# In the attention stage, the written order of the instructions is kept on two queues instead of five

## The chip, the cores and the metric

One core of one Trainium2 chip runs the whole program. The metric is the device time of one execution in microseconds (us); every time below is from that core. A core has five engines, each with an in-order queue: TensorE (PE in the profile; PEld is its weight load), VectorE (DVE), ScalarE (ACT), GpSimd (POOL) and SyncE (SP, which here only issues DMAs). An instruction at the head of a queue that waits for something holds everything behind it on that engine.

## The reference

Three steps follow one another. First a linear attention with random features (4 sequences of 576 tokens, 8 heads of 64, 128 features); then a mixture of experts that routes each token to one of 8 experts; then a gated FFN (SiLU of one product times another, times a third matrix). Cut to what matters:

```
phi(x): proj = x @ omega.T;  h = proj - sum(x*x)/2;  exp(h - max(h)) / sqrt(128)
kv = sum_s k_p[s] v[s];  z = sum_s k_p[s]
attention = (q_p @ kv) / (q_p @ z + 1e-6)
logits = normalise(x) @ normalise(expert_emb).T / tau;  idx = argmax;  gate = softmax(logits)[idx]
moe = gate * relu(x @ w1[idx]) @ w2[idx]
out = (silu(moe @ w_gate) * (moe @ w_val)) @ w_out
```

## The kernel before, in words

The 2304 tokens are 18 tiles of 128. The attention runs over 36 **units** (the list `units`, line 358), one tile of k or of q each: units 0 to 8 are nine k tiles, 9 to 17 the nine q tiles of the same two sequences (group 0), 18 to 26 and 27 to 35 the same for the other two sequences (group 1). A unit goes through these helpers:

- `load`: a DMA of the tile, 512 KB, from SP's queue. Four buffers, so the load of unit s+4 waits for the projection of unit s.
- `squares` (L391, for most q tiles also two halving adds L396, all on GpSimd), `norms` (L403, a sum on VectorE). Three `sq` buffers: the squares of a unit wait for the L403 three units before.
- `project` (L411, TensorE, 16 small matmuls into one of two PSUM pairs named `two`), `maxima` (L421 the maximum over PSUM, then the two short steps L425 and L428 in SBUF that make the bias; all on VectorE), `exps` (L437, eight activations on ScalarE, which then free the PSUM pair).
- k units then do `kv_sum` (L451, TensorE). q units do `turn` (L485, eight transposes into two PSUM banks `one`), `turned` (L490, one copy of a bank on VectorE and one on ScalarE), `numerators` (L503, TensorE, bank `third`, which needs both copies), `divide` (L514, L517, L518, VectorE; frees `third`), `token_norms` (L527, ScalarE), `turn_x` (L532, four transposes into a bank `one`, then the cast L535 on ScalarE) and `turned_x` (L539, VectorE).
- For every third q tile a piece of the router: `products` (L218), `products_out` (L225), `logits` (L230 into `third` in units 20 and 23, copied out by L233 on VectorE). Then, spread over the units by a generator that is advanced once a unit: the roots (L144 to L159, L210, L211), the softmax and gates (L242 to L272), and the counts (L288 to L307), which end in the index of the first expert (L300, `dom_i`).

The loop over `s` (lines 573 to 625) writes these stages down software-pipelined: in step s stand `turned`, `numerators` and `divide` of unit s-2, `turn_x` of unit s-3, `turn` or `kv_sum` of unit s-1, and the projection, maxima and exps of unit s itself. In the last steps it also fetches the first expert's weights (`first.fetch`, line 625): a DMA into `raw` whose address is read from `dom_i`, the cast L89 on ScalarE and the subtraction L90 on GpSimd. All of it lies in `tc.manual_schedule()`: inside it every engine issues its instructions in the order of the source. Outside it a list scheduler orders each engine, by its own estimates; the expert's matmuls (L671, then L691), which are written after the block, may be put between instructions of the block wherever the scheduler finds their inputs early enough. After the attention come the experts (to about 375 us) and the gated FFN (L865, L838).

Of the kernel before, what the change touches and what calls it, by code (L numbers as in the profile page):

```python
# [27 lines left out]
def attention_moe_ffn_kernel(  # L28
# [40 lines left out]
    def third():  # L69
        return psum.tile([128, 2, 512], F32, tag="third", name="third", bufs=1)  # L70
# [244 lines left out]
    ENG = mybir.EngineType  # L315
# [49 lines left out]
    with p1:  # L365
# [193 lines left out]

        with tc.manual_schedule():
            p = third()
            for _ in range(13):
                nc.tensor.matmul(p[:, 0, 0:128], ones, ones, start=True, stop=True)
# [386 lines left out]
```

## Time and profile before

| | |
|---|---|
| median of 3 runs | 823.15 us (822.75 to 823.5) |
| the profiled execution, its own time | 824.23 us |
| its span on the chip, first to last instruction | 822.5 us |
| busy: PE, PEld | 802.4 us (98%), 707.4 us (86%) |
| busy: DVE, ACT, POOL | 533.1 us (65%), 273.1 us (33%), 165.8 us (20%) |
| mean granted TensorE clock | 0.993 |

How to read it: busy time is the sum over the instructions of an engine. PE is busy nearly throughout, but a matmul that is fed slowly by a waiting weight also counts as busy, so a busy PE can still be held by another engine. The rows of the section before the prediction come from views of the trace: busy time in stretches, who waited for whom (the time an engine sat idle, its times, the longest), and the timeline (start, duration, engine, line, operation, output<-input, and in brackets the idle time before it and what ended it).

### The profile page before, as it was taken

Reading aid. Unit: us, or ns where it says so; the run is one execution under the profiler, and the core shown is the slowest. Engines: PE = TensorE matmul, PEld = TensorE weight load, DVE = VectorE, ACT = ScalarE, POOL = GpSimd, SP = SyncE. Lnnn points to the kernel's source line nnn. Section 1 sums busy time; section 2 is a strip of 40 time slices with the busy share of each in tenths; the row PEclk is TensorE's granted clock in tenths of the full one; section 3 lists DMA queues with packets and bytes.
Section 4 is the critical chain, followed back from the end, with each engine's and each line's share of the span. In section 5 each row is a group of like instructions: output and inputs, shape, how many; then the busy total and the mean of one; then the engine's idle time right before and its main releaser. Section 6 shows DMA issues by size and latency. Waiting matters only on the chain.

```text
span 822.5 us, 13988 instructions
## 1 busy us (share of the span) xinstructions
PE 802.4 (98%) x5734; PEld 707.4 (86%) x5735; DVE 533.1 (65%) x917; ACT 273.1 (33%) x628; POOL 165.8 (20%) x163
## 2 busy tenths in 40 slices
PE   8989989999999998999999999999999999999998
PEld 7778867899999998998888888888888888888886
DVE  5888899684333432689992059728954993797354
ACT  3678577642222324322224232112211221221120
POOL 4452253120000004412232111212111121112020
PEclk9999999999999998999999999999999999999999
DMA  7745652132423241332120002101110210020014
GB/s 282 210 115 174 185 170 72 61 117 82 100 92 92 79 92 55 103 93 87 53 76 26 1 27 77 52 1 52 51 52 1 78 55 22 26 78 26 1 52 179
DMA packets 23680, 66.71 MB, mean 81 GB/s; under 512 B 3104, under 2 KB 5680, under 8 KB 23608
## 3 DMA queue, kind: packets, MB, share of 16 engines
q1 hardware_dynamic: 23608, 65.74, 26.1%
q8 instruction: 46, 0.75, 0.4%
q14 instruction: 26, 0.21, 0.1%
HBM read 60.94 MB, written 4.79 MB: 80 GB/s over the span
## 4 chain that ended last, share of the span: by engine, by line
PE 60%; DVE 0%; issue 0%
PE two L865 24%; PE one L838 18%; PE third L865 12%; PE two L671 3%; PE third L691 2%; PE two L691 2%; PE third L671 1%; DVE y_acc L847 0%
## 5 line engine op out<-in xcount | busy, mean ns | idle before, releaser
L865 PE MATMUL two<-xp,wp 128*128 128x512 f32 (+1 forms) x960 | 209.5, 368 | 0.0
L865 PEld LDWEIGHTS two<-xp,wp 128*128 128x128 f32 x960 | 168.1, 188 | 31.4 <-DVE s L872 0.6
L838 PE MATMUL one<-wo,h 128*128 128x512 f32 x648 | 159.8, 390 | 0.0
L90 POOL TENSOR_TENSOR h<-s,h 128x512 fp32r<-128x512 f32 (+1 forms) x60 | 78.1, 1302 | 337.9 <-ACT h L89 337.9
L838 PEld LDWEIGHTS one<-wo,h 128*128 128x128 f32 x648 | 120.6, 188 | 24.8 <-DVE y_acc L847 0.3
L847 DVE TENSOR_TENSOR y_acc<-y_acc,one 128x512 f32<-128x512 f32 x90 | 61.5, 684 | 77.3 <-PE one L838 77.2
L865 PE MATMUL third<-xp,wp 128*128 128x512 f32 (+1 forms) x480 | 106.5, 368 | 0.0
L865 PEld LDWEIGHTS third<-xp,wp 128*128 128x128 f32 x480 | 84.4, 188 | 15.4
L437 ACT ACTIVATE ph<-two,bias 128x128 f32<-128x128 f32 x288 | 78.1, 384 | 33.6 <-DVE bias L428 26.2
L671 PE MATMUL two<-xp,wp 128*128 128x288 f32 x576 | 82.7, 302 | 3.7 <-DVEq L756 3.7
L671 PEld LDWEIGHTS two<-xp,wp 128*128 128x128 f32 x576 | 80.1, 194 | 4.0 <-ACT xp L89 3.9
L89 ACT CAST h<-s 128x512 fp32r<-128x512 f32 (+1 forms) x60 | 34.7, 579 | 77.7 <-DVE s L872 77.7
L89 ACT CAST wp<-raw 128x1024 fp32r<-128x1024 f32 x32 | 33.6, 1049 | 61.8 <-PE two L691 35.1
L872 DVE TENSOR_TENSOR s<-two,s 128x512 f32<-128x512 f32 (+1 forms) x40 | 25.3, 633 | 44.3 <-ACT s L871 44.2
L691 PE MATMUL third<-h,wp 128*128 128x288 f32 x384 | 52.5, 296 | 0.0
L691 PE MATMUL two<-h,wp 128*128 128x288 f32 x384 | 51.8, 296 | 0.0
L871 ACT ACTIVATE s<-two 128x512 f32<-128x512 f32 (+1 forms) x40 | 22.1, 552 | 89.0 <-PE two L865 89.0
L691 PEld LDWEIGHTS third<-h,wp 128*128 128x128 f32 x384 | 51.6, 189 | 0.0
L691 PEld LDWEIGHTS two<-h,wp 128*128 128x128 f32 x384 | 51.4, 189 | 0.0
L90 DVE TENSOR_TENSOR wp<-raw,wp 128x1024 fp32r<-128x1024 f32 x30 | 39.6, 1319 | 14.9 <-ACT wp L89 14.9
L90 POOL TENSOR_TENSOR xp<-y_f,xp 128x576 fp32r<-128x576 f32 x12 | 18.6, 1590 | 151.3 <-ACT xp L89 151.3
L421 DVE TENSOR_REDUCE mx<-two 128x8 f32<-128x1024 f32 x36 | 43.8, 1216 | 5.2 <-PE two L411 5.0
(150 smaller groups left out, 925.9 us busy)
## 6 DMA issues: line engine op xcount, KB each, us to landing
raw<-in_w_dram SPq DMA_DIRECT2D x68, 512.0 KB, 3.6
q<-in_qx_dram SPq DMA_DIRECT2D x18, 512.0 KB, 3.6
k<-in_kx_dram SPq DMA_DIRECT2D x17, 512.0 KB, 4.1
v<-in_vx_dram SPq DMA_DIRECT2D x18, 276.0 KB, 3.8
out_dram<-y_acc SPq DMA_DIRECT2D x18, 256.0 KB, 2.0
gate<-gts SPq DMA_DIRECT2D x4, 256.0 KB, 5.3
k<-in_kx_dram SPq DMA_DIRECT2D x2, 128.0 KB, 2.2
k<-in_kx_dram SPq DMA_DIRECT2D x1, 256.0 KB
```

The source lines that it names most:

```text
L89: nc.scalar.copy(hi, src)
L90: lo_eng.tensor_tensor(out=lo, in0=src, in1=hi.bitcast(F32), op=ALU.subtract)
L421: nc.vector.tensor_reduce(out=mx.rearrange("p (c a) -> p a c", a=2), in_=p.rearrange("p a (h m) -> p a h m", m=M), axis=AX.X, op=ALU.max,)
L437: nc.scalar.activation(out=ph[:, h, :], in_=p[:, h % 2, h // 2 * M:(h // 2 + 1) * M], func=AF.Exp, bias=bias[:, h:h + 1],)
L671: nc.tensor.matmul(ps[:, j], w[:, a, c, f * 128:(f + 1) * 128], xp[:, c, b, c0 + j * HB:c0 + (j + 1) * HB], start=(c == 0 and n == 0), sto ...
L691: nc.tensor.matmul(ps[:, j], w[:, a, f, :], h[:, b, j * HB:(j + 1) * HB], start=(f == 0 and n == 0), stop=(f == len(hs) - 1 and n == 2),)
L838: nc.tensor.matmul(p, h[:, x, i * 128:(i + 1) * 128], w[:, a, :], start=(k == 0), stop=(k == 3 * GF - 1),)
L847: nc.vector.tensor_tensor(out=dst, in0=dst, in1=p, op=ALU.add)
L865: nc.tensor.matmul(ps[:, m], w[:, a, m, c, :], xp[:, c, x, cols], start=(k == 0), stop=(k == 3 * NC - 1),)
L871: nc.scalar.activation(out=s, in_=ps[:, 0], func=AF.Silu)
L872: nc.vector.tensor_tensor(out=s, in0=ps[:, 1], in1=s, op=ALU.mult)
```

## The change

```diff
-        with tc.manual_schedule():
+        with tc.manual_schedule(engines={ENG.PE, ENG.SP}):
             p = third()
             for _ in range(13):
                 nc.tensor.matmul(p[:, 0, 0:128], ones, ones, start=True, stop=True)
```

Inside the block TensorE's and SP's instructions keep the order of the source; those of ScalarE, VectorE and GpSimd are now placed by the list scheduler. The instructions themselves are the same. SP's order does not change at all, and TensorE's first change stands behind the projection of unit 35: from there on the first expert's matmuls (L671) stand earlier and in other places between the last units' steps. There is one other thing in that stretch: the last `turn_x` (unit 35) now stands directly behind the numerators of the same unit and three small L230, where before 21 matmuls L671 stood between. Three places show what moves. A name's number is the buffer; `ph` are the exps' outputs, `qt` the copies of a turned tile, `x` the divided tile, `mx` and `bias` the maxima and the exps' bias, `sh` the norms, `wp` and `raw` the expert's weights.

ScalarE at the first q unit (unit 9; `qt_691` is its copy, `ph_670` and `ph_714` are the exps of units 10 and 11). Before:

```order
L475 ACTIVATE kv1_646<-third_434 128x260
L437 ACTIVATE ph_670<-two_654,bias_666 128x128 x8
L490 COPY qt_691<-one_680 128x512
L437 ACTIVATE ph_714<-two_698,bias_710 128x128 x8
L490 COPY qt_757<-one_746 128x512
```

and with the change:

```order
L475 ACTIVATE kv1_646<-third_434 128x260
L490 COPY qt_691<-one_680 128x512
L437 ACTIVATE ph_670<-two_654,bias_666 128x128 x8
L437 ACTIVATE ph_714<-two_698,bias_710 128x128 x8
L490 COPY qt_757<-one_746 128x512
```

The copy of unit 9 now stands ahead of the exps of unit 10; that of unit 10 stays behind the exps of unit 11. The same is done at unit 27.

VectorE in a q unit (unit 14: `mx_940`; `one_932` is the turned x of unit 11, `r_973` and `x_972` the division of unit 12, `qt_914` and `qt_991` the copies of units 12 and 13). Before:

```order
L490 COPY qt_914<-one_902 128x512
L403 TENSOR_REDUCE sh_938<-sq_760 128x8
L421 TENSOR_REDUCE mx_940<-two_923 128x2x4
L425 SCALAR_TENSOR_TENSOR mx_940<-sh_938,mx_940 128x8
L428 SCALAR_TENSOR_TENSOR bias_941<-sh_938,mx_940 128x8
L539 TENSOR_TENSOR xp_97<-one_932,xp_97 128x4x128
L514 TENSOR_SCALAR r_973<-third_955 128x8
L517 RECIPROCAL r_973<-r_973 128x8
L518 TENSOR_TENSOR x_972<-third_955,r_973 128x512
```

and with the change:

```order
L403 TENSOR_REDUCE sh_1024<-sq_835 128x8
L517 RECIPROCAL r_898<-r_898 128x8
L490 COPY qt_914<-one_902 128x512
L518 TENSOR_TENSOR x_897<-third_880,r_898 128x512
L421 TENSOR_REDUCE mx_940<-two_923 128x2x4
L539 TENSOR_TENSOR xp_97<-one_932,xp_97 128x4x128
L425 SCALAR_TENSOR_TENSOR mx_940<-sh_938,mx_940 128x8
L428 SCALAR_TENSOR_TENSOR bias_941<-sh_938,mx_940 128x8
L514 TENSOR_SCALAR r_973<-third_955 128x8
L403 TENSOR_REDUCE sh_1101<-sq_917 128x8
L517 RECIPROCAL r_973<-r_973 128x8
L490 COPY qt_991<-one_977 128x512
```

L539 now stands ahead of L425 and L428, the copy L490 ahead of L518, and the norms L403 are those of the next unit.

ScalarE near the end of the attention (`ph_2258` are the exps of unit 33, `x_2192` the divided tile of unit 30, `one_2236` its turned form; the two L89 are the casts of the first expert's weights, which before stood behind the last exps, at units 36 and 37 of the loop). Before:

```order
L490 COPY qt_2207<-one_2198 128x512
L527 ACTIVATE x2_2214,ss_91<-x_2192 128x512
L535 CAST xp_97<-one_2236 128x4x128
L437 ACTIVATE ph_2258<-two_2216,bias_2254 128x128 x8
L490 COPY qt_2302<-one_2293 128x512
```

and with the change:

```order
L490 COPY qt_2207<-one_2198 128x512
L527 ACTIVATE x2_2214,ss_91<-x_2192 128x512
L89 CAST wp_2508<-raw_2506 128x1024
L535 CAST xp_97<-one_2236 128x4x128
L89 CAST wp_2547<-raw_2545 128x1024
L437 ACTIVATE ph_2258<-two_2216,bias_2254 128x128 x8
L490 COPY qt_2302<-one_2293 128x512
```

Both casts now stand ahead of the exps of unit 33, the first also ahead of the cast L535 of unit 30. On VectorE the small router steps, before spread over units 2 to 5 (expert embedding), 20 to 24 (roots) and 24 to 30 (softmax, gates), are now drawn together: the embedding's in units 0 to 2, the roots between L421 of unit 19 and L421 of unit 21, the softmax and gates all between the bias of unit 23 and L421 of unit 24. L233 of unit 20, before ahead of L421 of its unit, now stands behind it.

## Rows read from the trace of the kernel before

**Rows 1.** Busy time of each engine in two stretches: start:end, length, busy (x count)

```profile
0.00:171.10 171.10, 158.75 (x2170) 136.14 (x2172) 138.85 (x324) 116.03 (x377) 62.05 (x87) 0.99 0.50 157
171.10:317.00 145.90, 145.90 (x1094) 145.63 (x1092) 60.33 (x97) 37.15 (x47) 0.00 (x0) 1.00 0.32 87
```

**Rows 2.** Who PE waited for, 0 to 175 us: us in total, times, longest

```profile
PE third L503 <- ACT qt L490: 2.3, 2, 1.2
PE one L485 <- DVE xp L539: 1.5, 3, 0.8
PE one L532 <- DVE qt L490: 1.0, 1, 1.0
PE third L503 <- DVE qt L490: 0.7, 1, 0.7
PE third L503 <- DVE oc L258: 0.6, 1, 0.6
```

**Rows 3.** Timeline of PE at the first numerators (unit 9), their second half

```profile
46.73 0.88 PE L503 MATMUL third<-kv,qt 128*64 128x96 f32 x16 [1.17 <-ACT qt L490]
```

**Rows 4.** Timeline of ACT, then DVE, in one q unit of group 1

```profile
137.34 2.17 ACT L437 ACTIVATE ph<-two,bias 128x128 f32<-128x128 f32 x8 [0.84 <-DVE bias L428]
139.35 0.64 ACT L490 COPY qt<-one 128x512 f32<-128x512 f32 x1
...
140.44 0.64 ACT L535 CAST xp<-one 128x512 fp32r<-128x512 f32 x1
...
141.87 0.17 DVE L425 SCALAR_TENSOR_TENSOR mx<-sh,mx 128x8 f32<-128x8 f32 x1
...
142.16 0.68 DVE L539 TENSOR_TENSOR xp<-one,xp 128x512 fp32r<-128x512 f32 x1
```

**Rows 5.** Timeline of PE: the projections of units 12 and 19

```profile
48.57 1.16 PE L411 MATMUL two<-om_s,q 64*128 64x128 f32 x16
...
82.59 1.16 PE L411 MATMUL two<-om_s,k 64*128 64x128 f32 x16
```

**Rows 6.** Timeline of POOL and DVE around 36 us; a DMA row of the page

```profile
35.83 1.04 POOL L391 TENSOR_TENSOR sq<-q 128x512 f32<-128x512 f32 x1 [1.26 <-DMA q<-in_qx_dram]
...
35.95 0.94 DVE L425 SCALAR_TENSOR_TENSOR mx<-sh,mx 128x8 f32<-128x8 f32 x1
...
37.00 0.69 DVE L428 SCALAR_TENSOR_TENSOR bias<-sh,mx 128x8 f32<-128x8 f32 x1
...
q<-in_qx_dram SPq DMA_DIRECT2D x18, 512.0 KB, 3.6
```

**Rows 7.** Timeline: turn_x of unit 17 (PE), a softmax step (DVE); a group of the page

```profile
88.81 0.66 PE L532 MATMUL third<-ident,x 128*128 128x128 f32 x4 [0.30 <-DVE lg L233]
...
109.10 0.23 DVE L123 TENSOR_TENSOR cand<-lg,lm 128x72 f32<-128x72 f32 x1
...
L421 DVE TENSOR_REDUCE mx<-two 128x8 f32<-128x1024 f32 x36 | 43.8, 1216 | 5.2 <-PE two L411 5.0
```

**Rows 8.** The first expert's weights: index, DMA, landing (130 to 175 us), cast; PE's units 32, 33

```profile
140.37 0.15 DVE L300 CAST dom_i<-fst 1x2 int32<-1x2 f32 x1
...
141.23 0.91 SPq L343 DMA_DIRECT2D raw<-in_w_dram  x2
...
raw<-in_w_dram SPq DMA_DIRECT2D x6, 512.0 KB, 3.8
...
L89 ACT CAST wp<-raw 128x1024 fp32r<-128x1024 f32 x32 | 33.6, 1049 | 61.8 <-PE two L691 35.1
...
133.47 1.16 PE L411 MATMUL two<-om_s,q 64*128 64x128 f32 x16
...
143.12 1.09 PE L485 MATMUL one<-ident,ph 128*128 128x128 f32 x8
```

**Rows 9.** A router step beside GpSimd's last work (timeline of DVE and POOL)

```profile
166.19 2.51 DVE L144 TENSOR_SCALAR ny<-ss 128x9 int32<-128x9 int32 x1
...
166.63 2.04 POOL L755 MEMSET y_f<- 128x2304 f32 x1
```

## The prediction

> **What bounds the kernel now.** I read the busy times by stretch first. From 171.1 us to the branch at 317 us PE is busy for the whole 145.9 us, and the change does not touch the work there; in the first 171.1 us PE is busy 158.75 us, so it is idle for 12.35 us [rows 1]. That is all that another order could win if no other engine becomes slower, and part of it (the start, the first exps) is not a matter of order. So the effect is a question of few microseconds: 0.2% of this time, about what a measurement of this kernel can tell from no change, is 1.65 us. Then the waits of PE: few, and each with a place [rows 2]. Last the timelines, unit by unit, because TensorE keeps its order and only the arrival of what it waits for can change. In a q unit PE is nearly full: units 12 to 19 take 82.59 - 48.57 = 34.02 us, 4.86 us each [rows 5]. What stands close behind is the chain over ScalarE and VectorE.
>
> **The change part by part.** Each term is in us of PE's idle time, against the profiled execution of 824.23 us (1.73 us outside its span of 822.5 us, taken as unchanged), which stands 1.08 us above the median of 823.15 us.
>
> *a. The first numerators of group 0, -1.9.* PE waits for ScalarE's copy L490 of unit 9 because that copy stands behind the exps of unit 10; the numerators stop for 0.7 us for VectorE's half and then for 1.17 us for ScalarE's [rows 2, 3]. With the copy ahead of these exps both waits go: 1.87 us. Bounds: 0, if the next chain is late instead, and -2.7, if PE also gains what the exps of unit 9 lost to GpSimd [rows 6].
>
> *b. The pace of the q units, group 0, +2.2.* L539 now stands ahead of L425 and L428. That closes a loop through two engines in every q unit: from the start of the exps 2.01 us to L490, 1.09 us to L535, 0.64 us for it, then L539 with 0.68 us, L425 and L428 with 0.17 us each, then the next exps: 2.01 + 1.09 + 0.64 + 0.68 + 0.34 = 4.76 us [rows 4]. That equals PE's own 4.86 us, so by itself it costs nothing, but it has no slack left. What then decides is GpSimd. L425 took 0.94 us instead of 0.17 and L428 0.69: each ended as an instruction of GpSimd ended (35.83 + 1.04 = 36.87; L425 ended at 36.89) [rows 4, 6]. While GpSimd computes squares these two steps stand still. Before, the squares mostly waited for L403; now L403 runs a unit ahead, and the squares of unit s+4 start as soon as their tile lands, 3.6 us after an issue that follows the projection of unit s [rows 6]. At the head of a q group, where a projection waits for the exps two units before to free its PSUM pair, it ends 1.16 us after them [rows 5]; L425 comes no sooner than 2.01 + 1.09 + 0.64 + 0.68 = 4.42 us after that same moment, the two steps end at 4.42 + 0.34 - 1.16 = 3.6 us after the projection: just as the squares start. Any delay makes them meet, and then the next unit is late too, so the meeting repeats until no more q tile is loaded. I put two meetings (units 12 and 13) at 1.1 us each, one L391 of 1.04 us and the wait to get in. Bounds: 0, and twice 0.94 + 0.69 - 0.34 = 1.29 us, the delay of these two steps around 36 us [rows 6].
>
> *c. The router's steps drawn together, +0.5.* L233 of unit 20 now stands behind L421 with its 1.2 us, and PE's turn_x of unit 17, which waited 0.30 us for L233 [rows 7], waits about 0.9 us more. Some 15 steps of 0.23 us at most [rows 7] and one L403 stand ahead of L421 of unit 24: near 3.8 us, of which I estimate that 2 make its exps late, the rest being time in which VectorE waited for the projection. But the same steps are then gone from units 25 to 30, where the exps are late today. Bounds 0 and +2.9; I take +0.5, near the lower end, since the VectorE time as a whole is the same.
>
> *d. The first numerators of group 1, -2.6.* The same as in a, at unit 27: 0.6 + (2.3 - 1.17) = 1.7 us, and of the 1.5 us that L485 waits for L539 the longest wait, 0.8, which comes from the gates' steps that now are earlier [rows 2]. Bounds 0 and -3.2 (all of the 1.5).
>
> *e. The pace of the q units, group 1, +3.3.* As in b: two meetings that are not there before, at units 30 and 31, 2.2 us; bounds 0 and 2.6. Besides, the gates' transpose L292 needs a bank that ScalarE's L490 of unit 30 frees, and that copy stands behind exps of 2.17 us [rows 4], now with nothing else for PE to do; I take half of them, 1.1 us, between 0 and 2.2.
>
> *f. The weights' casts, +1.2.* From the projection of unit 32 to the turn of unit 32 PE now takes 143.12 - 133.47 - 1.16 = 8.5 us [rows 8]. In the new order, from the same point: L421 with 1.2 us, nine short steps near 0.2 us and L539 with 0.68 us to the end of L300 [rows 4, 7], 3.7 us; 0.7 us to the DMA's issue and 3.8 us to its landing; then L89 with 1.05, L535 with 0.64 and L539 with 0.68, since the turn needs the bank that these two free [rows 4, 8]: 3.7 + 0.7 + 3.8 + 2.4 = 10.6 us. So 2.1 us late; what e takes away from PE's lead lies in the same stretch, so I take 1.0, and 0.2 for the exps of unit 33, which now also stand behind the second cast. Bounds 0 and 2.1. The casts themselves, 2 x 1.05 us, lie on ScalarE and would be hidden if the weights were there.
>
> *g. The end, +0.6.* The wait of 1.0 us of L532 for a copy [rows 2] goes, since expert matmuls stand there now. The last L532 stands directly behind its unit's numerators and needs three short steps of VectorE near 0.2 us [rows 7] and L518, 512 columns as L539 with its 0.68 us [rows 4]: 1.3 us, of which the small L230 cover 0.1: +1.2. The first L671 needs the pair that the exps of unit 34 free, +0.4. Bounds -1.0 and +1.0.
>
> GpSimd's other moves (four memsets) and the embedding's steps, drawn together in units 1 to 3, cost nothing: there the tiles' DMAs end GpSimd's waits, and the steps only change places within VectorE's time; if that cover were gone it would be ten steps of up to 0.2 us, 2 us.
>
> Sum: -1.9 + 2.2 + 0.5 - 2.6 + 3.3 + 1.2 + 0.6 = +3.3 us: 827.5 us for the profiled execution, 826.4 us at the level of the median.
>
> *A rule weighed.* L144, a step with one input, ended at 168.70 us, with GpSimd's memset at 168.67 us [rows 9]; the other router steps ran in 0.2 us. The Trainium skill, "SBUF — State Buffer", section "Who interferes with whom", says that such one-input steps too can take the port pair that VectorE shares with GpSimd, that the one who starts first keeps it for the whole instruction, and the other blocks fully. The rows agree for L425, L428 and L144. By the rule the roots' steps drawn together behind unit 19 could meet the squares once more, which would be one L391 more than in my sum, 1.0 us; by the rows of undisturbed steps it is nothing.
>
> **The rivals.**
> 1. *GpSimd's squares stay clear of L425 and L428.* Once settled, the loop of 4.76 us leaves the squares, which land late, behind both steps. Then b is 0 and e is 1.1: -1.9 + 0.5 - 2.6 + 1.1 + 1.2 + 0.6 = -1.1 us, 822.1 us, not slower; with c at 0 and f at 0 besides, -2.8 us, 820.4 us. For it: today's squares of q tiles mostly wait for L403, so their landing is not seen to hurt. Against it: the margin is nil at the head of each group. It decides whether L428 ends less or more than 3.6 us after its unit's projection.
> 2. *The meetings repeat in every unit whose squares are of q tiles that land during q units.* Three more at 1.1 us: +6.6 us, 829.7 us. For it: a late L425 makes the next one late. Against: PE also slows then, and so does the next load.
> 3. *Gain and loss cancel.* PE's order is kept, its work is the same, and 158.75 of 171.1 us are PE's own; with slack that I do not see, the moved steps hide and a, d stand against f, g and half of e: within 1 us, 823 us.
>
> **How the numbers follow.** Forecast (a to g as summed) 0.48; its own range by half of its bounds is 824.8 to 828.4 us. Rival 1: 0.27, about half of it beyond 0.2%. Rival 2: 0.10. Rival 3: 0.15. Faster by over 0.2%: 0.27 x 0.5 and a little of rival 3, 0.16. Within 0.2%: the rest of rival 1, most of rival 3 and the forecast's lower edge, 0.28. Slower: 0.56. The range that leaves out 2 in 10 goes from rival 1 between its two values, 821.3, to rival 2, 829.6 us.
>
> **What would show it.** Right: no wait of L503 for L490 at units 9 and 27; L535, L539, L425, L428, exps in a row in every q unit, at 4.8 us or more; L425 or L428 at 0.5 us and more beside L391 in units 12, 13, 30 and 31; ScalarE idle for 1 us or more in front of the first L89, ended by the weights' DMA; PE idle for about 1 us in front of the last L532. Wrong: L425 and L428 at 0.17 us in all q units (then rival 1), or the expert's matmuls that follow 171 us no longer without gaps.

## The result, and the profile after

The changed kernel takes 829.67 us (median of 5 runs, 827.81 to 830.91) against 823.15 us (5 runs): a ratio of 1.0073, 95% interval 1.0059 to 1.0088, so 4.9 to 7.2 us **slower**. The profiled execution took 829.67 us with a span of 827.9 us, 5.4 us more than that of before; the mean granted clock is 0.987 against 0.993. Forecast were 826.4 us and, for the profiled execution, 3.3 us more than before; the median lies 0.07 us above the upper end of the range, 829.6 us.

The windows of the two stretches that answer to [rows 1] (start:end, length, then PE, PEld, DVE, ACT, POOL busy with counts, granted clock, DMA share, GB/s):

```profile
0.00:171.10 171.10, 153.35 (x2073) 132.05 (x2074) 130.76 (x306) 112.58 (x369) 60.00 (x86) 0.96 0.50 157
171.10:317.00 145.90, 144.68 (x1150) 143.86 (x1149) 64.14 (x114) 40.08 (x54) 2.02 (x1) 1.00 0.31 87
```

In the first stretch TensorE is idle for 17.75 us instead of 12.35, and its clock is 0.96 instead of 0.99. Who it waited for, from 0 to 185 us (us in total, times, longest):

```profile
PE one L451 <- ACT ph L437: 4.2, 1, 4.2
PE one L532 <- DVE x L518: 3.6, 7, 1.2
PE third L451 <- ACT ph L437: 2.8, 3, 2.0
PE third L532 <- DVE lg L233: 2.4, 1, 2.4
...
PE one L292 <- ACT qt L490: 0.9, 1, 0.9
...
PE one L485 <- DVE xp L539: 0.7, 2, 0.5
```

The waits of L503 for the copies L490 [rows 2, 3] are gone, as forecast in a and d. In their place stand a longer first wait for the exps, seven waits for L518, and two waits of some 2 us, for L233 and for the exps of unit 24.

Since TensorE keeps its order, its **lateness** can be read at the start of each unit's projection (after minus before). It is 1.8 us at unit 11, 0.3 at 13, 2.3 at 20, 5.9 at 21, 6.7 at 28, 8.1 at 35, and at the first L691 (the expert's second matmuls, 189.02 us before) 8.4 us:

| stretch of the attention | forecast | measured in the change | the same piece alone (experiments below) |
|---|---|---|---|
| start, to unit 11 | 0 | +1.8 | +2.8 |
| units 11 to 13 (a) | -1.9 | -1.5 | -1.2 |
| units 13 to 20 (b) | +2.2 | +2.0 | +1.6; +0.2 (two halves) |
| unit 20 to 21 (c, L233) | +0.9 | +3.6 | +3.0 |
| units 21 to 28 (c, gates) | -0.4 | +0.8 | +2.9 |
| units 28 to 35 (d, e, f) | +1.9 | +1.4 | |
| unit 35 to the first L691 (g) | +0.6 | +0.3 | |
| sum | +3.3 | +8.4 | |

Of 8.4 us TensorE then regains 3.1 within the experts, by a faster pace of its matmuls whose cause is not settled (last section), so that the span is 5.4 us longer.

**The start.** Timeline (start, duration, engine, line, operation, in brackets the idle time before and its releaser):

```profile
9.20 0.16 DVE L177 RECIPROCAL rtau<-rtau 128x1 f32<-128x1 f32 x1 [2.06 <-DMA rtau<-in_tau_dram]
9.27 0.63 ACT L178 ACTIVATE e<-es 8x512 f32<-8x512 f32 x1 [7.22 <-DMA es<-in_emb_dram]
...
10.03 0.14 DVE L144 TENSOR_SCALAR ny<-ess 8x1 int32<-8x1 int32 x1
10.10 1.20 DVE L421 TENSOR_REDUCE mx<-two 128x8 f32<-128x1024 f32 x1
...
12.36 2.83 PE L451 MATMUL one<-v,ph 128*64 128x96 f32 x32 [4.23 <-ACT ph L437]
```

Two steps of 0.1 and 0.2 us, whose results TensorE first needs at 56.04 us (the transposes L188), stand ahead of the first maxima and wait for small DMAs; VectorE stands still for 2.06 us with the maxima behind them. Before, the same L421 began at 7.51 us, and TensorE's first wait for the exps was 1.65 us shorter:

```profile
10.94 2.45 PE L451 MATMUL one<-v,ph 128*64 128x96 f32 x32 [2.58 <-ACT ph L437]
```

**A q unit.** The starts of units 12 and 19 on PE, which answer to [rows 5], 36.64 us apart instead of 34.02; then one unit over all engines, which answers to [rows 4]:

```profile
48.22 1.16 PE L411 MATMUL two<-om_s,q 64*128 64x128 f32 x16
...
84.86 1.16 PE L411 MATMUL two<-om_s,k 64*128 64x128 f32 x16
```

```profile
62.99 2.17 ACT L437 ACTIVATE ph<-two,bias 128x128 f32<-128x128 f32 x8 [1.03 <-DVE bias L428]
...
63.92 0.68 DVE L518 TENSOR_TENSOR x<-third,r 128x512 f32<-128x512 f32 x1
...
64.75 0.63 PE L532 MATMUL one<-ident,x 128*128 128x128 f32 x4 [0.27 <-DVE x L518]
...
66.09 0.65 ACT L535 CAST xp<-one 128x512 fp32r<-128x512 f32 x1
66.77 0.69 DVE L539 TENSOR_TENSOR xp<-one,xp 128x512 fp32r<-128x512 f32 x1 [1.02 <-ACT xp L535]
...
67.38 0.16 DVE L425 SCALAR_TENSOR_TENSOR mx<-sh,mx 128x8 f32<-128x8 f32 x1
...
67.92 0.14 DVE L428 SCALAR_TENSOR_TENSOR bias<-sh,mx 128x8 f32<-128x8 f32 x1
68.10 2.17 ACT L437 ACTIVATE ph<-two,bias 128x128 f32<-128x128 f32 x8 [1.36 <-DVE bias L428]
```

The forecast's loop is there (L535, L539, L425, L428, exps in a row), 5.11 us from exps to exps. But L425 and L428 take 0.14 to 0.17 us in all of units 12 to 19: no meeting with the squares. There were meetings with GpSimd before, which the prediction does not count, with the halving adds L396: L425 took 0.50, 0.67 and 0.33 us in units 12 to 14, and L428 0.43 us in unit 12 and 0.43 to 0.64 us in units 28 to 32. Unit 13, before:

```profile
55.70 1.28 POOL L396 TENSOR_TENSOR sq<-sq 128x256 f32<-128x256 f32 x2
55.79 0.67 DVE L425 SCALAR_TENSOR_TENSOR mx<-sh,mx 128x8 f32<-128x8 f32 x1
```

So in units 12 to 19 the change took meetings away instead of adding them. The loop is longer than 4.76 us because a small step may stand within it (here the copy L225, 0.54 us) and because L535 comes late.

**Units 20 and 24**, in the timeline that answers to [rows 7]:

```profile
91.08 0.17 DVE L144 TENSOR_SCALAR ny<-ss 128x9 int32<-128x9 int32 x1 [1.22 <-ACT x L527]
...
91.83 1.22 DVE L421 TENSOR_REDUCE mx<-two 128x8 f32<-128x1024 f32 x1
92.97 0.20 DVE L233 COPY lg<-third 128x48 f32<-128x48 f32 x1
...
93.22 1.11 PE L532 MATMUL third<-ident,x 128*128 128x128 f32 x4 [2.44 <-DVE lg L233]
...
94.26 2.57 PE L451 MATMUL one<-v,ph 128*64 128x96 f32 x32
...
113.36 2.77 PE L451 MATMUL third<-v,ph 128*64 128x96 f32 x32 [1.99 <-ACT ph L437]
```

and the window behind the first of these waits:

```profile
93.20:96.80 3.60, 3.58 (x38) 3.13 (x38) 3.43 (x14) 2.66 (x9) 1.04 (x1) 0.55 0.18 73
```

Again a step that waits, L144 for ScalarE's sum of squares, stands ahead of the maxima and of L233. TensorE idles 2.44 us; in the 3.6 us that follow, its granted clock is 0.55, so most of them at the lower level of 1.2 GHz, and 32 matmuls L451 take 2.57 us where 1.54 is usual. At unit 24 the burst of gate steps in front of the maxima meets GpSimd as well, which adds some 0.9 us to it: the second of two steps L263, 0.16 us each before, ends with the squares.

```profile
109.37 1.20 DVE L263 TENSOR_TENSOR oc<-oc,oh 64x8 f32<-64x8 f32 x2
109.50 1.04 POOL L391 TENSOR_TENSOR sq<-q 128x512 f32<-128x512 f32 x1 [1.73 <-DVE se L268]
```

**Unit 27**, in the timeline that answers to [rows 6]:

```profile
121.44 1.04 POOL L391 TENSOR_TENSOR sq<-q 128x512 f32<-128x512 f32 x1 [3.04 <-DVE mx L421]
121.47 1.03 DVE L425 SCALAR_TENSOR_TENSOR mx<-sh,mx 128x8 f32<-128x8 f32 x1
...
122.61 0.70 DVE L428 SCALAR_TENSOR_TENSOR bias<-sh,mx 128x8 f32<-128x8 f32 x1
```

Here L425 meets the squares and L428 the halving adds; at units 28 and 29 they still take 0.38 to 0.43 us in part, later 0.17. The next projection that needs a free pair, that of unit 29, is 1.3 us later for it.

**The end**, which answers to [rows 8]:

```profile
148.91 1.05 ACT L89 CAST wp<-raw 128x1024 fp32r<-128x1024 f32 x1 [1.64 <-DMA raw<-in_w_dram]
...
178.88 0.63 PE L532 MATMUL one<-ident,x 128*128 128x128 f32 x4 [1.22 <-DVE x L518]
```

Both are as forecast: ScalarE idle for 1.6 us in front of the cast (above 1 us was expected), and the last L532 waits 1.22 us (1.2).

### The profile page after: what moved, and what is told of

Read it like the earlier page. It is cut to its first block, busy times and chain, and to the rows that moved or that the text cites. A ratio compares the mean times of both kernels' runs of the same rounds, so it can differ in the third digit from the quotient of the medians.

```text
span 827.9 us, 14028 instructions
## 1 busy us (share of the span) xinstructions
PE 801.1 (97%) x5734; PEld 706.9 (85%) x5735; DVE 529.7 (64%) x917; ACT 273.0 (33%) x628; POOL 165.8 (20%) x163
## 4 chain that ended last, share of the span: by engine, by line
PE 60%; issue 0%; ACT 0%; DVE 0%; ACTq 0%
PE two L865 24%; PE one L838 18%; PE third L865 12%; PE two L671 3%; PE third L691 2%; PE two L691 2%; PE third L671 1%; ACT xp L89 0%; DVE y_acc L847 0%; ACTq L89 0%
## 5 line engine op out<-in xcount | busy, mean ns | idle before, releaser
L90 POOL TENSOR_TENSOR h<-s,h 128x512 fp32r<-128x512 f32 (+1 forms) x60 | 78.1, 1302 | 337.9 <-ACT h L89 337.9
L671 PE MATMUL two<-xp,wp 128*128 128x288 f32 x576 | 82.2, 301 | 4.2 <-ACT xp L89 3.8
L671 PEld LDWEIGHTS two<-xp,wp 128*128 128x128 f32 x576 | 79.3, 194 | 4.6 <-ACT xp L89 4.0
L89 ACT CAST h<-s 128x512 fp32r<-128x512 f32 (+1 forms) x60 | 34.7, 579 | 77.4 <-DVE s L872 77.4
L89 ACT CAST wp<-raw 128x1024 fp32r<-128x1024 f32 x32 | 33.5, 1046 | 60.7 <-PE two L691 34.1
L691 PE MATMUL third<-h,wp 128*128 128x288 f32 x384 | 51.7, 293 | 0.0
L691 PE MATMUL two<-h,wp 128*128 128x288 f32 x384 | 50.9, 293 | 0.0
L691 PEld LDWEIGHTS third<-h,wp 128*128 128x128 f32 x384 | 50.8, 188 | 0.0
L691 PEld LDWEIGHTS two<-h,wp 128*128 128x128 f32 x384 | 50.5, 188 | 0.0
L421 DVE TENSOR_REDUCE mx<-two 128x8 f32<-128x1024 f32 x36 | 44.0, 1221 | 7.9 <-PE two L411 7.5
L90 DVE TENSOR_TENSOR wp<-raw,wp 128x1024 fp32r<-128x1024 f32 x30 | 39.0, 1300 | 14.7 <-ACT wp L89 14.6
L90 POOL TENSOR_TENSOR xp<-y_f,xp 128x576 fp32r<-128x576 f32 x12 | 18.6, 1594 | 145.5 <-ACT xp L89 145.5
```

Source lines behind the costliest of these rows:

```text
L89: nc.scalar.copy(hi, src)
L90: lo_eng.tensor_tensor(out=lo, in0=src, in1=hi.bitcast(F32), op=ALU.subtract)
L421: nc.vector.tensor_reduce(out=mx.rearrange("p (c a) -> p a c", a=2), in_=p.rearrange("p a (h m) -> p a h m", m=M), axis=AX.X, op=ALU.max,)
L671: nc.tensor.matmul(ps[:, j], w[:, a, c, f * 128:(f + 1) * 128], xp[:, c, b, c0 + j * HB:c0 + (j + 1) * HB], start=(c == 0 and n == 0), sto ...
L691: nc.tensor.matmul(ps[:, j], w[:, a, f, :], h[:, b, j * HB:(j + 1) * HB], start=(f == 0 and n == 0), stop=(f == len(hs) - 1 and n == 2),)
```

## Experiments

Each experiment was timed beside before. Lateness always means the start of a projection or of the first L691 against the profiled execution of before. In kernels that leave the start as it was, it differs by up to 1.6 us in the first units and by up to 0.7 us at unit 11; behind unit 13 such differences stay, so its growth from unit to unit is what counts. In kernels with added lines, later line numbers are shifted by a few.

**1. The start alone.**

```diff
                     norms(s)
+                    if s == 0:
+                        next(router)
+                        next(router)
                     maxima(s)
```

> The written order of before, with one piece of the new order: the embedding's first steps (L177, L178, L144, L148) stand ahead of the first maxima. Theory A (read from the two profiles): these steps wait for their DMAs until about 9.2 us and hold the first maxima and exps; unit 2's projection starts near 15.1 us instead of 13.3, most of it is still there at unit 8, and the whole run is 1 to 2 us slower. Theory B (the prediction's: the k units' own waits cover the embedding's steps): unit 2 may be late, but by unit 11 the starts are within 0.5 us of before, and the run is the same within 0.5 us.

Ratio 1.0027 (1.0017 to 1.0038), 2.2 us. Unit 2 is 2.9 us late, unit 11 2.8, unit 35 2.8.

```profile
13.48 2.83 PE L451 MATMUL one<-v,ph 128*64 128x96 f32 x32 [3.49 <-ACT ph L437]
```

So the price of the embedding's steps is not covered by anything and is carried unchanged through the whole attention. The prediction's zero falls. Its 2 us "if that cover were gone" come near in size by luck: they were the sum of ten short steps, and what is lost is a wait for DMAs.

**2. L518 behind the next copy.** `divided` is the step L518, which `divide` no longer issues.

```diff
                     turned(s - 2)
+                if tile_of(s - 3, "q") is not None:
+                    divided(s - 3)
                 if s + 2 < N:
                     squares(s + 2)
```

> The written order of before, with one piece of the new order: the division's last step L518 of a q unit stands behind VectorE's copy L490 of the next unit (one step later) instead of ahead of it; L539 stays behind L428. Theory A (read from the two profiles): the turn_x of TensorE then waits 0.3 us and more for L518 in most q units; units 12 to 19 take about 36.5 us instead of 34.0, no L425 or L428 is lengthened there, and with the same in the second group the run is 3 to 5 us slower. Theory B (the prediction's: pace is lost only where L425 and L428 stand behind L539 and meet the squares): nothing of that is in this kernel, units 12 to 19 stay at 34.0 us, within 0.5, and the run is within 0.8 us of before.

Ratio 1.0001 (0.9990 to 1.0012), units 12 to 19 in 34.30 us. Theory A falls: L518 behind the copy costs next to nothing by itself. The seven waits for L518 in the change are where the lateness shows; experiment 6 has this piece together with the other.

**3. Unit 20 alone.**

```diff
                     norms(s)
+                    if s == 2 * PT + 2:
+                        next(rest)
                     maxima(s)
...
                 in_=p.rearrange("p a (h m) -> p a h m", m=M), axis=AX.X, op=ALU.max,
             )
+            if s == 2 * PT + 2:
+                route[0].logits_out(1)
```

> The written order of before, with one piece of the new order at unit 20: the first root steps (L144, L148), which wait for ScalarE's sum of squares of unit 17, ahead of the maxima L421 of unit 20, and the copy of the logits behind it. Theory A (read from the two profiles): TensorE idles 2 us or more in front of the turn_x of unit 17, the granted clock is low in the next 3 us (single matmul groups 1.6 times as long), and unit 21 starts 3 to 4 us later than in before; the run is 2.5 to 4 us slower. Theory B (the prediction's size): about 0.9 us at unit 21 without any change of the clock.

Ratio 1.0051 (1.0038 to 1.0064), 4.2 us, a little above theory A's 4. Lateness goes from 0.4 at unit 20 to 3.4 at unit 21; 1.1 us more are lost between units 29 and 31, for a reason that was not followed up. The turn_x of unit 17 in the timeline:

```profile
90.79 0.75 PE L539 MATMUL third<-ident,x 128*128 128x128 f32 x4 [1.91 <-DVE lg L238]
```

and the window behind it:

```profile
90.79:94.30 3.51, 3.51 (x38) 3.02 (x38) 1.48 (x4) 2.67 (x9) 0.74 (x1) 0.56 0.31 121
```

Theory A holds. Of the 3.0 us, 1.6 are the longer wait (1.91 against 0.30 in [rows 7]); most of the rest is the clock, 0.56 in the window behind the wait.

**4. The gates' steps at unit 24.**

```diff
-                if base >= 1:
+                for _ in range({2: 2, 4: 7}.get(base, base == 1 or base == 3 or base > 11)):
                     next(rest, None)
```

> The written order of before, with one piece of the new order: all softmax and gate steps of the first group stand ahead of the maxima of unit 24, and are gone from units 25 to 30. Theory A (read from the two profiles): TensorE idles about 2 us in front of the kv product at unit 24 or 25, runs at the lower granted clock after it, and unit 26 starts about 2 us later; in units 27 to 30 at most 1 us of it comes back, so the run is 1 to 2 us slower. Theory B (the prediction's): 2 us are lost at unit 24 and 1.5 to 2 us come back in units 25 to 30, where the same steps no longer stand; the run is within 0.6 us of before.

Ratio 1.0055 (1.0036 to 1.0074), 4.5 us, more than either theory allowed. From unit 21 to 28 the lateness grows by 2.9 us. TensorE's kv product behind the wait:

```profile
109.03 2.59 PE L451 MATMUL third<-v,ph 128*64 128x96 f32 x32 [3.08 <-ACT ph L437]
```

and the window from there:

```profile
109.00:113.50 4.50, 4.46 (x50) 3.90 (x50) 2.15 (x5) 3.92 (x15) 3.08 (x4) 0.62 0.05 19
```

Here 18 steps stand in a row in front of the maxima, the last two of the roots among them, against 15 in the change, and TensorE waits 3.08 us instead of 1.99; 0.6 us of the 3.5 lost at unit 26 had come back by unit 28. The prediction's "gone from units 25 to 30, where the exps are late today" did not pay back what the burst cost. In this profiled execution the branch behind the attention happened to cost little (last section); the timed runs scatter from 824.3 to 831.4 us, with a mean granted clock of 0.996 at the one end and 0.985 at the other.

**5 and 6. L539 ahead of the bias, alone and with L518 behind the copy.** The diff is that of 5; 6 adds that of 2.

```diff
                 in_=p.rearrange("p a (h m) -> p a h m", m=M), axis=AX.X, op=ALU.max,
             )
+            if tile_of(s - 3, "q") is not None:
+                turned_x(s - 3)
...
-                if old is not None:
+                if old is not None and s >= N:
                     turned_x(s - 3)
```

> The written order of before, with one piece of the new order: VectorE's L539 stands between the maxima L421 and the two bias steps in every q unit; L518 stays ahead of the next copy. Theory A (formed after the experiment with L518 alone): L539 ahead of the bias closes a loop of 4.8 us through ScalarE and VectorE, still under TensorE's 4.86 us, so alone it costs little: units 12 to 19 take 34.0 to 35.0 us, the run is within 1.5 us of before. Theory B (the prediction's): the two bias steps come later and meet the squares at units 12, 13, 30 and 31 (0.5 us or more for L425 or L428), 1.1 us each, and the run is 3 to 5 us slower.

> The two pieces together: L539 ahead of the bias steps, and L518 behind the next unit's copy L490. Theory A: now one loop runs through L490, L518, TensorE's turn_x L532, ScalarE's L535, L539, the bias steps and the exps, near 5.1 to 5.2 us against TensorE's 4.86: units 12 to 19 take 36 to 37 us, TensorE waits 0.3 us in front of most L532, no bias step is lengthened in units 14 to 19, and the run is 4 to 6 us slower. Theory B (meetings alone): as with L539 alone. Theory C (neither counts, the pace was lost to the norms of the next unit that also stood ahead): within 1 us of before.

Ratios 1.0023 (1.0012 to 1.0034) and 1.0021 (1.0005 to 1.0036), 1.9 and 1.7 us. From unit 13 to 20 the lateness grows by 1.6 us in 5 and 2.0 in 6, the change's own 2.0; units 12 to 19 take 35.37 and 35.46 us. L425 takes 0.15 to 0.17 us in units 13 to 19 of both, so nothing meets. The loss also falls at the same units as in the change (0.9 us at unit 16, 0.4 at 18, 0.3 to 0.4 at 19). So it comes from L539 ahead of the bias by itself: neither from the squares, nor from the longer loop through L518 that theory A had formed (6 should have stood well behind 5). But 5 and 6 had gained 1.1 and 1.4 us between units 11 and 13, where the wait of L503 for VectorE's half of the copies and one of L485 for L539 are gone; from unit 11 to 20 they lose only 0.5 and 0.6 us. How much of the change's -1.5 in units 11 to 13 is this gain, and how much the head's, was not separated.

**7. The two heads alone.** At units 10 and 28, `turn` and `turned` of the unit before stand ahead of `exps`; the later calls skip these units.

```diff
                     maxima(s)
+                    if s in (PT + 1, 3 * PT + 1):
+                        turn(s - 1)
+                        turned(s - 1)
                     exps(s)
```

> The written order of before, with only the piece that was priced as a gain: at units 10 and 28 the turn and the two copies of the first q unit of a group stand ahead of the next unit's exps on ScalarE. Theory A: TensorE's two waits of L503 for the copies go at each head (1.9 us at unit 11, 1.7 us at unit 29), about 1.5 us of each stays to the end, and the run is 2.5 to 4 us faster, 819.5 to 821 us. Theory B (the gain is given back, since the next chain is late instead): unit 12 starts 1.5 us or more earlier, but unit 16 less than 0.7 us, and the run is within 1 us of before.

Ratio 0.9970 (0.9956 to 0.9983): 2.5 us **faster**. Unit 12 starts 1.99 us early (1.85 gained from unit 11), unit 13 1.30, and so it stays; at unit 30 1.39 more are gained from unit 29 and 0.65 given back at 31. So a and d are real, and a third to a half of each is given back one unit later.

**8 and 9. One engine's order free.**

```diff
-        with tc.manual_schedule():
+        with tc.manual_schedule(engines={ENG.PE, ENG.SP, ENG.DVE, ENG.Pool}):
```

> The change for ScalarE alone (TensorE, SP, VectorE and GpSimd keep the written order). Theory A: the two heads gain as in the kernel with only the heads (3 us together), and what was lost at the start came from VectorE's queue, so the start is within 0.7 us of before; the casts of the first expert's weights cost under 1 us here; the run is 1 to 3.5 us faster. Theory B (the loss of the change is ScalarE's: the embedding's L178 first at the start, the casts ahead of the exps at the end): unit 2 starts 1 us or more late, ScalarE waits 1 us or more for the weights, and the run is slower by 1 us or more.

For the other, `ENG.Activation` stands in place of `ENG.DVE`.

> The change for VectorE alone (TensorE, SP, ScalarE and GpSimd keep the written order). Theory A (the losses are VectorE's queue, the gains ScalarE's): 2 to 3 us late at unit 2 because L177 waits for its DMA ahead of the first maxima, no gain at units 12 and 30, 1.3 to 2.5 us lost over units 12 to 19, 3 to 4 us at unit 21, about 2 us at unit 24 to 26: together the attention's end is 9 to 12 us late, the run 6 to 11 us slower, so that this and the run with ScalarE alone (2.6 us faster) add up to the change within 2 us. Theory B (the engines' new orders only hurt together): under 3 us slower. For the pace of the experts' matmuls (24 in 3.12 us in the change, 3.20 us in before): if it comes with VectorE's or TensorE's new order at the end of the attention, it shows here too.

With ScalarE free: 0.9968 (0.9954 to 0.9982), 2.6 us faster. With VectorE free: 1.0147 (1.0124 to 1.0171), 12 us slower, more than the 6 to 11 that were expected. The first of these is not what it looks like. With ScalarE alone TensorE is 3.0 us early at unit 34, but 0.2 late at unit 35 and 2.3 late at the first L691; the run is faster because its experts' matmuls have the faster pace of the last section, worth 3.1 us. So the time that theory A expected came by luck. With VectorE alone the first L691 is 14.5 us late, at the slower pace. In the attention, then, ScalarE's order is a gain up to unit 34 that its end takes away again, and VectorE's is a loss.

The two don't add up: 9.5 us in time, not the change's 6, outside the 2 us that were expected, and 16.8 us of lateness at the first L691, where the change has 8.4. Of this difference 2.6 us are there at unit 11: with VectorE alone it is 5.8 us late, with ScalarE alone 1.4 early, in the change 1.8 late. In the change ScalarE's L178 comes first and draws the 1.28 us of the exps' table load to 0.8 us, in the shadow of VectorE's wait; with VectorE alone the load still follows the first bias, and L177 began 1.3 us later. Most of the rest arises behind unit 28, where VectorE alone loses 3.6 us to the first L691, ScalarE alone 4.9 and the change 1.7. At the end ScalarE's order does lose what f says: behind the projection of unit 34 the second cast waits for its DMA ahead of L535, and TensorE for what follows,

```profile
144.57 1.04 ACT L89 CAST wp<-raw 128x1024 fp32r<-128x1024 f32 x1 [1.24 <-DMA raw<-in_w_dram]
...
147.49 1.12 PE L485 MATMUL one<-ident,ph 128*128 128x128 f32 x4 [2.53 <-DVE xp L539]
```

and 3.2 us are lost from unit 34 to 35, more than the "under 1 us" that was expected.

**10. The end written.** The change, with the loop cut in two blocks; `step(s)` is the loop's body:

```diff
+        with tc.manual_schedule(engines={ENG.PE, ENG.SP}):
...
+            for s in range(0, 30):
+                step(s)
+        with tc.manual_schedule():
+            for s in range(30, N + 3):
+                step(s)
```

> The change, but from unit 30 of the loop on all five queues keep the written order again. Theory A (terms f and g): up to unit 30 as in the change (5.9 us late there, within 1 us), after it the 2.2 us that units 32 to 35 lost and the 1.2 us of the last turn_x do not come; the first L691 stands 2 to 3.5 us earlier than in the change. Theory B: the end costs nothing by itself, since TensorE only takes up what VectorE left: the first L691 is within 1 us of the change's. The run is 2 to 3.5 us faster than the change by A if the experts' matmuls keep the pace of 3.12 us for 24, and about as slow as the change if they fall back to 3.20 us, which takes 3.1 us.

Ratio 1.0063 (1.0049 to 1.0078). From unit 31 to the first L691 nothing more is lost (4.50 and 4.51 us), where the change loses 2.1: f and g are there, and belong to the new order. The first L691 is 3.9 us earlier than in the change; part of that is not the end's (unit 30 is 2.5 us earlier, since some of the gates' steps fell behind the cut). The experts' matmuls are back at the slower pace of the last section (24 in 3.20 us instead of 3.12), which takes away 3.1 us; so the run gains 0.9 us only.

**11. Heads and table load.** Experiment 7, and one instruction:

```diff
+            warm = wk.tile([128, 1], F32, name="warm", bufs=1)
+            nc.scalar.activation(out=warm, in_=ones[:, 0:1], func=AF.Exp)
             p = third()
```

> The written order with the two heads as in the earlier experiment, and one added ScalarE instruction of one column at the program's start, whose only use is that the table load of 1.28 us, which stands behind the first bias in before, lies in the first microseconds. Theory A (read from the run with ScalarE alone, where unit 6 starts 1.5 us earlier): 1.3 us at unit 2 and still at unit 9, with the heads' 2.0 together 3.3 us: 819 to 820.5 us. Theory B (the start is bound by the tiles' DMAs): unit 9 within 0.3 us of before, and the run as with the heads alone, 0.3% faster.

Ratio 0.9953 (0.9939 to 0.9967), 819.84 us: 3.9 us faster than before, the best of all.

```profile
0.78 1.28 ACT L564 ACT_TABLE_LOAD   x1 [0.64 <-PEq L941]
...
9.24 2.19 PE L451 MATMUL one<-v,ph 128*64 128x96 f32 x32 [1.10 <-ACT ph L437]
```

TensorE waits 1.10 us for the first exps instead of 2.58; unit 9 starts 2.3 us early and unit 35 4.8. Theory A holds; more than its 1.3 us shows at unit 9 in this execution.

**12. The start written.** As 10, with the blocks the other way round:

```diff
+        with tc.manual_schedule():
...
+            for s in range(0, 4):
+                step(s)
+        with tc.manual_schedule(engines={ENG.PE, ENG.SP}):
+            for s in range(4, N + 3):
+                step(s)
```

> The change, but in the first four steps of the loop all five queues keep the written order; behind them as in the change, and TensorE's order is the change's throughout. Theory A (the start's loss is L177 and L144 waiting for their DMAs ahead of the first maxima): unit 11 starts within 0.6 us of before instead of 1.8 us late, the rest of the attention loses what it loses in the change, so the first L691 is 6 to 7 us late instead of 8.4. Theory B (the loss at the start is taken up later anyway): the first L691 is as late as in the change. The experts' matmuls: if their faster pace belongs to TensorE's order at the end of the attention (a transpose L292 behind the seventh L691), 24 take 3.12 us here too and the run is 827 to 828.5 us; if it was chance, 3.20 us and 830 to 831.5 us.

Ratio 1.0068 (1.0043 to 1.0092), 828.11 us. Unit 11 is 0.2 us late instead of 1.8, so the start's loss is gone and stays gone up to unit 31 (2.9 us late instead of 6.3, more than the start alone explains). Most of the rest is the clock. At unit 20 TensorE waits 2.44 us here just as in the change, but the granted clock of the window behind the wait is 1.00:

```profile
91.22 0.66 PE L532 MATMUL third<-ident,x 128*128 128x128 f32 x4 [2.44 <-DVE lg L233]
91.81 1.54 PE L451 MATMUL one<-v,ph 128*64 128x96 f32 x32
```

```profile
91.20:94.80 3.60, 3.58 (x54) 3.18 (x55) 3.29 (x16) 2.67 (x9) 1.04 (x1) 1.00 0.29 89
```

From unit 20 to 21 2.1 us are lost, where the change loses 3.6: 1.5 us of that row are the clock, which does not fall behind every wait of this length. The prediction's meetings at units 30 and 31 do come here, beside L391 (L425 with 1.04 and 0.82 us), and between units 30 and 32 1.4 us are lost; which part of it is theirs was not separated. Then 3.4 us are lost from unit 32 to 33: TensorE waits 1.24 us in front of L292, as e said, and 0.44 behind it, and between those units its granted clock is 0.80. The first L691 is 7.0 us late instead of 8.4. What an earlier stretch wins can be lost by a later wait and the clock drop behind it.

## Why the prediction was right or wrong, point by point

The sign was right, and the time 3.3 us too low in the medians, 2.2 in the profiled executions. That is closer than the reasons were: the sum for the attention was 5.1 us too low, and the experts became 3.1 us faster, which no term held. That the result lies at rival 2's 829.7 us is no evidence for it: its repeated meetings are not there.

- **a and d, the heads: right in mechanism, too large.** The waits of L503 are gone. In the change the first head gives 1.5 us (2.2, then 0.6 back), alone 1.2, where 1.9 was taken; the second gives 1.7 us in the change (2.0, then 0.4 back), alone 0.7, where 2.6 was taken (1.7 of it for these waits; the two parts of that sum make 2.5). What failed is "both waits go: 1.87 us" without what is late next; the bound of 0 named that case.
- **b, the pace of group 0: right in size, wrong in cause.** Forecast +2.2, measured +2.0. "By itself it costs nothing" is the step that failed: with L539 ahead of the bias and no meeting in units 13 to 19, experiment 5 loses 1.6 us between units 13 and 20 (behind a gain of 1.1). The 4.76 us were the sum of rows at their shortest, against 4.86 us of TensorE; the loop ran at 5.11 us where other small steps stood in it. Of the "two meetings (units 12 and 13)" none came; the sign named for rival 1, both steps at 0.17 us, is there in units 12 to 19, but its price of nothing is not.
- **e, the pace of group 1:** the meeting came, but once and at unit 27 (1.3 us), not at units 30 and 31, where it came in experiment 12. That such meetings "are not there before" is wrong as well: L428 took 0.52 and 0.58 us beside L396 in these two units before. Behind the first four steps VectorE's order is the same in the change and in experiment 12, so which units meet is set by the timing that comes out of the start, which the prediction did not work out. L292 waited for the copy as forecast, 0.9 us and 0.44 behind it (forecast 1.1). Unit 27's L425 ended at 122.50 us, L391 at 122.48. The Trainium skill, "SBUF — State Buffer", section "Who interferes with whom", says that a VectorE instruction with two SBUF inputs contends with a GpSimd instruction that reads SBUF, and that the issue order decides who blocks; these rows agree. The extra meeting that the rule would have put on the roots behind unit 19 came as one step, L154, with 0.85 us at 95.08 us beside L391, while TensorE was busy; L263 at unit 24 met L391 ahead of a wait of TensorE. For L144 the prediction's "the rows agree" is not shown: in rows 9 L144 starts at 166.19 us, before the memset at 166.63 us with which it ends, and GpSimd's subtraction L90 runs until 166.70 us.
- **c, the router's steps: wrong, the largest error (+0.5, measured +4.4).** Two steps of it failed. L233 was costed by its place (0.9 us behind L421), but the new order also put L144 ahead of L421, and L144 waits for another engine: what matters of a moved step is what it waits for, not its 0.17 us. And "the VectorE time as a whole is the same" says nothing of when: the burst's loss was not given back in units 25 to 30. On top came what the forecast had no term for: behind the idle times of 2.44 and 1.99 us TensorE ran for some microseconds mostly at its lower clock. At unit 20 that is 1.5 of the 3.6 us, by experiment 12, where the clock did not fall behind the same wait; so this part is chance.
- **The embedding's steps: wrong (0, measured +1.8, alone +2.8).** "There the tiles' DMAs end GpSimd's waits" is no cover: the steps wait for DMAs of their own, that land at 9.2 us, and the first maxima stand behind them.
- **f and g: right.** Forecast +1.2 and +0.6; from unit 33 to 35 1.1 us were lost and from there to the first L691 0.3, at the rows that were named; experiment 10 takes both away.

The prediction's own range "by half of its bounds", 824.8 to 828.4 us, does not come out of them as they stand: half of all bounds, added up, is 5 us to either side.

What stays open: which of the steps ahead of the bias sets the loop's length unit by unit in b, since neither half alone reaches 5.1 us in every unit; what gives the experts' matmuls their faster pace; and how the terms of the change add up, since the two engines' parts don't.

## What to carry to other kernels

A list scheduler that orders by its own estimates may put steps with slack ahead of steps without any, as here; on an in-order queue a step of 0.2 us that waits for a DMA or another engine costs the whole wait to everything behind it, so of each moved step ask first what it waits for. Where an order is written by hand, look for single places where a free order is better and copy those: here two swaps and an early table load are worth 3.9 us, the free order as a whole costs 6.5. Price an idle time of TensorE of 2 us with the clock drop that can follow it, here 1.5 us at unit 20 and nothing in experiment 12. And before a gain is put down to an order, look whether it arose where the order was changed: with ScalarE alone it did not.

## What the runs showed of the hardware that was not expected

**The experts' matmuls have two paces.** At a granted clock of 1.00 and without a gap, 48 matmuls of 288 columns start 6.40 us apart in before and 6.24 us in the change. Timeline of PE, before:

```profile
195.42 12.96 PE L691 MATMUL two<-h,wp 128*128 128x288 f32 x96
...
320.87 9.10 PE L671 MATMUL two<-xp,wp 128*128 128x288 f32 x48 [3.69 <-DVEq L756]
```

and after:

```profile
203.78 12.64 PE L691 MATMUL two<-h,wp 128*128 128x288 f32 x96
...
326.29 9.14 PE L671 MATMUL two<-xp,wp 128*128 128x288 f32 x48 [3.79 <-ACT xp L89]
```

That is 133.3 and 130.0 ns each, constant over some 960 matmuls, 3.1 us in all. Three kernels have the faster pace up to the branch at 320 us: the change and experiments 8 and 12. They are the three whose TensorE order has L292 behind the seventh L691; the other eleven have it ahead of the first. Behind the branch, experiments 6, 7 and 12 have it, the change and 8 do not. So a stretch without gaps seems to keep the pace that it fell into; what decides it is not settled. The Trainium skill, "TensorE: Matmul & The Clock Gate", section "Wait — 56ns, not 53.3ns?", gives the columns at 2.4 GHz and some 2.5 ns, 122.5 ns by an estimate; neither pace here agrees.

**The clock after the branch differs between executions.** TensorE waits 3.7 to 4.0 us there in every kernel. The 48 matmuls that follow took 9.10 and 9.14 us above, but in experiment 4

```profile
323.41 6.62 PE L671 MATMUL two<-xp,wp 128*128 128x288 f32 x48 [3.68 <-DVEq L756]
```

6.62 us, as long as at full clock, and 7.8 to 9.1 us in the others. So 2.5 us lie between executions whose work there is the same; what decides it was not tested. The span of one execution says little about a change of this size.
